# Channel attention and a top-1 mixture of experts: split weights in two places by turns, the first split two steps later, the first v loads spread over the steps of rows, one batch's first squares freed

## The chip, the cores and the metric

One Trainium2 chip, one of its cores, one program. The metric is device time in microseconds of one execution; the time of a kernel is the median of its runs. Inputs and output are float32 in the chip's memory.

## The reference

```python
def _attn_ref(q, k, v, tau):                    # B, N, C = 4, 5056, 256
    qn = q / (np.linalg.norm(q, axis=1, keepdims=True) + 1e-06)
    kn = k / (np.linalg.norm(k, axis=1, keepdims=True) + 1e-06)
    s = kn.transpose(0, 2, 1) @ qn / tau        # 256 x 256 for each batch
    a = softmax(s)                              # over the last axis
    return v @ a

def _moe_ref(x, w_gate, w_output_gate, w1, w2): # x: 20224 x 256; E = 8, F = 1024
    logits = x @ w_gate
    e_idx = np.argmax(logits, axis=1)
    probs = softmax(logits)
    gate_w = probs[np.arange(N), e_idx]
    eom = 1.0 / (1.0 + np.exp(-(x @ w_output_gate)))
    for e in range(E):
        mask = e_idx == e
        h = np.maximum(x[mask] @ w1[e], 0.0)
        out[mask] = gate_w[mask, None] * eom[mask, e, None] * (h @ w2[e])

def reference(q, k, v, tau, **moe):
    return _moe_ref(_attn_ref(q, k, v, tau).reshape(20224, 256), **moe)
```

q and k are normalised along the 5056 rows, so a batch's 256 x 256 product can be scaled after it is summed. Each of the 20224 rows then goes through the one expert of eight that its logits choose.

## The kernel before, in words

The five engines and their queues are TensorE (PE, matmuls), VectorE (DVE), ScalarE (ACT), GpSimd (POOL, which issues the indirect transfers) and SyncE (SP, which issues the direct ones). SP and POOL issue in the order of the program; a row that waits holds up all rows behind it.

**Attention.** `gram(b)` goes over one batch in 20 steps of 256 rows. A step loads its rows of q and k (L406, tile `qk`, six of them), squares them on ACT (L390), adds the squares up on DVE (L391), and multiplies on PE into `s_ps` (L429). Behind the last step the product is copied from PSUM to `s_sb` (L438), scaled and made into the softmax. `mix(b)` then goes over the rows of v: `turn` loads v (L537, half a MB each, tile `v`), PE transposes (L543) and multiplies with the softmax (L573 to L575), `st` gets the result, and `route` sends each row into the place of its expert in the buffer `xs_d`, with scatters by POOL (L651). The batches overlap: while `mix` of batch b runs, `gram` of the next one does, and some of the first v loads are issued in it.

**Experts.** The experts are ranked by their number of rows, and the sorted rows are worked off in units of 256. A unit's first product `h_part` (L996 to L998) has 48 matmuls in four steps of 12, its `hb` (ReLU on ACT, L1000, and the rest on DVE, L1001) follows for each step, and its second product `y_part` (L1020 to L1022) goes by steps as well, a unit behind; a step of the run has 12 matmuls of each kind, 24 in all. PE works in float16 with each number as a sum of two parts, high and low, hence three matmuls for one product. A unit's rows are fetched (`xg`, L918), scaled and split into `xr16` (L970, L971; one tile of tag "sq" for a pair of units, two such tiles), and transposed by transfers on SP's queue (`xt`, L975). Its result `yo` (L1026) is stored by POOL (L1033). The h products and the small product `w_ps` below use one set of four PSUM tiles.

**Weights.** Each expert's w1 and w2 are split into the two parts once. `prep` does it for ranks 1 to 7 while the run goes on: for each half (half 0 is w1, half 1 is w2) `load_raw` loads 1 MB on SP (L288) into a tile of tag "st", which the scatters must have left; `split` squares it on ACT in two pieces (L333), DVE sums (`wtot`, L338), PE multiplies by ones (`w_ps`, L339) so that each partition has the total, the scale follows, and ACT makes the high part (`whi`, L354), DVE the low part (`wlo`, L355). `keep` writes both to `wsc` in the chip's memory (L363, half a MB each, on SP). Units fetch their expert's weights from there into `wbuf` (L889, POOL). Rank 0 is split ahead of the run, in `wbuf` itself, and units 0 to 6 use it; units 7, 13, 20, 26, 33, 39 and 46 are the first that may need ranks 1 to 7.

The parts lie in one tile each, of tags "sp" and "sl" with one buffer; so a split may begin only when the `keep` before it has been written out.

**Order.** Code is written by generators that take turns, and a scheduler places each engine's instructions by simulated times. `_beside(run, (preps, rate))` advances the preps by `rate` of a step for each step of the run: SRATE for the first 20 steps, WRATE (0.45) behind them. `pause(n)` gives n turns away. `issue_after` and `behind` hold an instruction behind another one on its engine; `in_turn` holds each piece of a split behind the run's last piece on ACT, DVE and PE. `AHEADW` = 2 is how many loads of weights stand ahead of the split that is worked on.

Of the kernel before, what the change touches and what calls it, by code (L numbers as in the profile page):

```python
# [9 lines left out]
F16 = mybir.dt.float16  # L10
BF16 = mybir.dt.bfloat16
F32 = mybir.dt.float32
# [26 lines left out]
def tile_colnorm_attention_then_top1_moe(  # L39
# [87 lines left out]
    LATE = 12  # L127
    MWAIT = 12
    BRATE = 0.7
    SOON, SRATE = 20, 0.9  # L130
    WRATE = 0.45
    WAITW = 1
    RWAIT = 3
    SMALL = 9
    VAFTER = 6
    AHEADW = 2
# [152 lines left out]
        return raw  # L289

    held = []

    def prep(first, end, tag):
        todo = []
        for r in range(first, end):
            for half in range(2):
                with behind("SP"):
                    raw = load_raw(r, half, tag)
                todo.append(lambda raw=raw, half=half, r=r: in_turn(split(raw, half, r), "ACT", "DVE", "PE"))
                yield  # L300
                if len(todo) > AHEADW:
                    yield from todo.pop(0)()
        for f in todo:
            yield from f()
# [17 lines left out]
    def split(raw, half, r):  # L322

        rows = slice(r * P, (r + 1) * P)
        if r == 0:
            hi, lo = (wbuf[half][:, 0, n * HW1 : (n + 1) * HW1] for n in range(2))
        else:
            hi = big.tile([P, HW1], F16, tag="sp", name=f"whi{r}_{half}", bufs=1)
            lo = big.tile([P, HW1], F16, tag="sl", name=f"wlo{r}_{half}", bufs=1)
        ss = sm.tile([P, 2], F32, tag="wss", name="wss")  # L330
        for i in range(2):
            a = slice(i * HW1 // 2, (i + 1) * HW1 // 2)
            nc.scalar.activation(hi[:, a], raw[:, a], AF.Square, accum_out=ss[:, i : i + 1])  # L333
            yield
        yield from pause(WAITW)
        w_ps = ps_x.tile([P, 512], F32, tag="x", name="w_ps")
        tot = sm.tile([P, 1], BF16, tag="wtot", name="wtot")
        nc.vector.tensor_tensor(out=tot, in0=ss[:, 0:1], in1=ss[:, 1:2], op=ALU.add)  # L338
        nc.tensor.matmul(w_ps[:, 0:1], onesb, tot, start=True, stop=True)  # L339
        sw = sm.tile([P, 1], F32, tag="wsw", name="wsw")  # L340
        root2(w_ps[:, 0:1], KW, sw, invw[:, half, r : r + 1])

        if half == 0:
            src, dh, dl = (
                raw.rearrange("p (c m f) -> p c f m", c=CC, f=FC),
                hi.rearrange("p (c f m) -> p c f m", c=CC, f=FC),
                lo.rearrange("p (c f m) -> p c f m", c=CC, f=FC),
            )
            cuts = [(slice(None), c, slice(i, i + FC // 2)) for c in range(CC) for i in (0, FC // 2)]
        else:  # L350
            src, dh, dl = raw, hi, lo
            cuts = [(slice(None), slice(i * HW1 // 2, (i + 1) * HW1 // 2)) for i in range(2)]
        for i, a in enumerate(cuts):
            nc.scalar.activation(dh[a], src[a], AF.Copy, scale=sw)  # L354
            nc.vector.scalar_tensor_tensor(  # L355
                out=dl[a], in0=src[a], scalar=sw, in1=dh[a], op0=ALU.mult, op1=ALU.subtract
            )
            if i % 2:
                yield
        def keep():  # L360
            with behind("SP"):
                for n, part in enumerate((hi, lo)):
                    nc.sync.dma_start(wsc[half][rows, n * HW1 : (n + 1) * HW1], part)  # L363

        if r == 0:
            held.append(keep)
        else:
            keep()
        if half == 1:
            iw = invw[:, :, r : r + 1]  # L370
            nc.vector.tensor_tensor(out=iw[:, 0, :], in0=iw[:, 0, :], in1=iw[:, 1, :], op=ALU.mult)
            prepped.append(r)
# [5 lines left out]
    def gram(b):  # L378
# [14 lines left out]
        for st in range(nstep):  # L393
            t0 = TS * st
            last = st == nstep - 1
            qk = ld.tile([P, 2, TS, C], F32, tag="qk", name=f"qk{b}_{st}", bufs=QKB)
            for i, src in enumerate((q, k)):
                main = src[b, :MAIN].rearrange("(p t) c -> p t c", p=P)
                nt = TS - 1 if last else TS
                if last and REM < P:  # L400
                    nc.vector.memset(qk[REM:, i, TS - 1, :], 0.0)
                if b == 0 and st == 0:
                    for t in range(nt):
                        (nc.sync, nc.scalar)[i].dma_start(qk[:, i, t, :], main[:, t, :])
                    continue
                load = nc.sync.dma_start(qk[:, i, :nt, :], main[:, t0 : t0 + nt, :])  # L406
                if b == 1 and st == VAFTER:
                    mile["rows"] = load
                if last:
                    nc.sync.dma_start(qk[:REM, i, TS - 1, :], src[b, MAIN:])  # L410
            for t0 in range(0, TS, 2):
                qp = qk[:, :, t0 : t0 + 2, :]
                if not last:
                    with ExitStack() as held_back:
                        if st < 2 and "copy" in mile:
                            held_back.enter_context(tc.issue_after(mile["copy"].ins))
                        squares(st, t0, qp)
                if b in WHOLE:
                    terms = [(qp, qp)]
                else:  # L420
                    hi = wk.tile([P, 2, 2, C], F32R, tag="qkh", name=f"qkh{b}_{st}_{t0}")
                    nc.scalar.copy(hi, qp)
                    lo = wk.tile([P, 2, 2, C], F32R, tag="qkl", name=f"qkl{b}_{st}_{t0}")
                    nc.vector.tensor_tensor(out=lo, in0=qp, in1=hi.bitcast(F32), op=ALU.subtract)
                    terms = [(hi, hi), (hi, lo), (lo, hi)]
                for t in range(2):
                    for c in range(CC):
                        for n, (kt, qt) in enumerate(terms):
                            nc.tensor.matmul(  # L429
                                s_ps[:, c, :], kt[:, 1, t, c * P : (c + 1) * P], qt[:, 0, t, :],  # L430
                                start=st == 0 and t0 == 0 and t == 0 and c == 0 and n == 0,
                                stop=last and t0 == TS - 2 and t == 1 and n == len(terms) - 1,
                                skip_group_check=True,
                            )
                yield
# [90 lines left out]
    def turn(b, j):  # L526
# [3 lines left out]
        if i % 2 == 0:  # L530
# [2 lines left out]
            vt = ld.tile([P, 4, C], F32, tag="v", name=f"v{b}_{g}_{i}", bufs=VB)  # L533
            with ExitStack() as held_back:
                if b == 0 and g < 2:
                    held_back.enter_context(tc.issue_after(mile["rows"].ins))
                main(SP=nc.sync.dma_start(vt[:np_], vg[:, 2 * i : 2 * i + 4, :]))  # L537
            sts["v"] = vt
        vp = sts["v"][:, 2 * (i % 2) : 2 * (i % 2) + 2, :]
# [618 lines left out]
```

## Time and profile before

| | us |
|---|---|
| median of three runs | 1213.61 (1211.7 to 1219.58) |
| the profiled execution | 1205.79 |
| its span | 1204.0 |
| PE busy | 1172.7 (97%) |
| DVE busy | 710.7 (59%) |
| ACT busy | 625.5 (52%) |
| POOL busy | 565.5 (47%) |

The granted clock of TensorE was 0.995 over the span. The profiled execution is 7.8 us under the median of the runs. Attention and routing take about the first 366 us, with the run of the experts beginning beside its end; the rest is the run. In rows of the profile, L12 is line 12 of the kernel; a wait is put down to the semaphore that came last; numbers of tiles are left out of names, so `raw` is any of the weights' loads, and `whi` any of the high parts.

### The profile page before, as it was taken

To read this page: it belongs to the slowest core of one execution; us is meant where nothing else is said; L and a number is where in the kernel's file an instruction comes from. 1 tells how busy PE (TensorE), PEld (TensorE's weight loads), DVE (VectorE), ACT (ScalarE), POOL (GpSimd) and SP (SyncE) were. 2 spreads that over 40 slices of the span, in tenths; PEclk is the share of its full clock that TensorE was granted. 3 is DMA by queue.
4 is the path that set the end of the run, shared out by engine and by line. 5 is a ranking of instruction groups with operands and counts; after the bars stand their busy time and mean duration, and the time that the engine had idled before them with its cause. 6 is when DMAs were issued, how large, how long until landed. Compare 5 with 4: busy or idle time off the path is not lost.

```text
span 1204.0 us, 27760 instructions
## 1 busy us (share of the span) xinstructions
PE 1172.7 (97%) x10412; PEld 1061.5 (88%) x10412; DVE 710.7 (59%) x2123; ACT 625.5 (52%) x1233; POOL 565.5 (47%) x561
## 2 busy tenths in 40 slices
PE   8999999999898899999999999999999999999998
PEld 7899899999787788888888888888889999999997
DVE  6676757758895655465565656544445555555551
ACT  5576757657746555465555555433333344344442
POOL 0004574767575235544444554445555544444443
PEclk9999999999999899999999999999999999999999
DMA  8986787847689855665655545733335433337843
GB/s 301 326 294 226 254 273 252 301 153 266 191 256 295 211 151 151 147 147 151 139 147 150 139 126 158 195 77 77 77 69 170 116 73 80 77 78 205 183 115 131
DMA packets 174882, 208.54 MB, mean 173 GB/s; under 512 B 120936, under 2 KB 124526, under 8 KB 169752
## 3 DMA queue, kind: packets, MB, share of 16 engines
q1 hardware_dynamic: 130312, 126.58, 37.3%
q0 software_dynamic: 43312, 79.73, 22.9%
q8 instruction: 84, 1.38, 0.5%
q14 instruction: 54, 0.44, 0.1%
q10 hardware_dynamic: 1120, 0.42, 0.1%
HBM read 275.55 MB, written 61.41 MB: 280 GB/s over the span
## 4 chain that ended last, share of the span: by engine, by line
PE 64%; issue 16%; DMA 8%; POOL 7%; ACT 3%; DVE 1%; POOLq 0%; SPq 0%; ACTq 0%; DVEq 0%
PE s_ps L429 8%; PE h_ps L996 8%; PE h_ps L998 8%; PE h_ps L997 8%; PE y_ps L1020 8%; PE y_ps L1022 8%; PE y_ps L1021 8%; POOL out_dram L1033 4%; DMA qk<-in_k_dram 2%; PE x_ps L573 2%; PE x_ps L575 2%; PE x_ps L574 2%; PE vt_ps L543 2%; POOL wbuf L889 2%; DMA xs_d<-st,r_si 2%
## 5 line engine op out<-in xcount | busy, mean ns | idle before, releaser
L1001 DVE SCALAR_TENSOR_TENSOR hb<-h_ps,hb 128x512 f16<-128x512 f32 (+1 forms) x360 | 227.8, 636 | 330.3 <-ACT hb L1000 329.9
L1000 ACT ACTIVATE hb<-h_ps 128x512 f16<-128x512 f32 (+1 forms) x360 | 196.9, 551 | 341.3 <-PE h_ps L998 340.9
L996 PE MATMUL h_ps<-xt,wbuf 128*128 128x256 f16 (+1 forms) x1440 | 367.9, 263 | 3.7 <-ACT st L576 2.0
L998 PE MATMUL h_ps<-xt,wbuf 128*128 128x256 f16 (+1 forms) x1440 | 368.0, 263 | 0.0
L997 PE MATMUL h_ps<-xt,wbuf 128*128 128x256 f16 (+1 forms) x1440 | 367.8, 263 | 0.0
L1020 PE MATMUL y_ps<-wbuf,hb 128*128 128x256 f16 x1296 | 353.4, 273 | 1.1 <-DMA wbuf<-wsc,wi 1.1
L1021 PE MATMUL y_ps<-wbuf,hb 128*128 128x256 f16 x1296 | 353.4, 273 | 0.0
L1022 PE MATMUL y_ps<-wbuf,hb 128*128 128x256 f16 x1296 | 353.2, 273 | 0.0
L889 POOL DMA_INDIRECT wbuf<-wsc,wi x166 | 168.9, 1018 | 221.0 <-PE h_ps L998 163.1
L651 POOL DMA_INDIRECT xs_d<-st,r_si x160 | 173.0, 1081 | 180.5 <-ACT st L576 106.1
L1033 POOL DMA_INDIRECT out_dram<-yo,b_id x162 | 166.7, 1029 | 69.0 <-issue 41.2
L996 PEld LDWEIGHTS <-wbuf 128*128 128x128 f16 x1440 | 141.4, 98 | 18.8 <-DMA wbuf<-wsc,wi 2.6
L997 PEld LDWEIGHTS <-wbuf 128*128 128x128 f16 x1440 | 141.4, 98 | 14.7 <-issue 0.4
L429 PE MATMUL s_ps<-qk 128*128 128x256 f32 x640 | 148.1, 384 | 5.9 <-DMA qk<-in_q_dram 3.9
L998 PEld LDWEIGHTS <-wbuf 128*128 128x128 f16 x1440 | 141.4, 98 | 14.1
L1021 PEld LDWEIGHTS <-hb 128*128 128x128 f16 x1296 | 126.7, 98 | 15.3 <-issue 1.2
L1022 PEld LDWEIGHTS <-hb 128*128 128x128 f16 x1296 | 126.7, 98 | 14.9 <-DVE hb L1001 0.2
L1020 PEld LDWEIGHTS <-hb 128*128 128x128 f16 x1296 | 126.7, 98 | 14.2 <-ACT hb L1000 0.3
L429 PEld LDWEIGHTS s_ps<-qk 128*128 128x128 f32 x640 | 119.6, 192 | 21.4 <-DMA qk<-in_k_dram 3.9
L905 POOL DMA_INDIRECT xg<-xs_d,gi x49 | 50.8, 1036 | 155.2 <-DVE xr L971 145.8
L391 DVE TENSOR_TENSOR acc<-acc,sq 128x1024 f32<-128x1024 f32 x76 | 92.9, 1223 | 36.9 <-ACT sq L390 29.8
L390 ACT ACTIVATE sq<-qk 128x1024 f32<-128x1024 f32 x76 | 80.1, 1061 | 44.7 <-DMA qk<-in_k_dram 39.1
(195 smaller groups left out, 1488.4 us busy)
## 6 DMA issues: line engine op xcount, KB each, us to landing
qk<-in_q_dram SPq DMA_DIRECT2D x75, 256.0 KB
qk<-in_k_dram SPq DMA_DIRECT2D x75, 256.0 KB
v<-in_v_dram SPq DMA_DIRECT2D x32, 512.0 KB
raw<-in_moe_w_dram SPq DMA_DIRECT2D x16, 1024.0 KB
xg<-xs_d SPq DMA_DIRECT2D x30, 272.0 KB
wsc<-whi SPq DMA_DIRECT2D x14, 512.0 KB
wsc<-wlo SPq DMA_DIRECT2D x14, 512.0 KB
v<-in_v_dram SPq DMA_DIRECT2D x8, 480.0 KB
```

The source lines that it names most:

```text
L429: nc.tensor.matmul(s_ps[:, c, :], kt[:, 1, t, c * P : (c + 1) * P], qt[:, 0, t, :], start=st == 0 and t0 == 0 and t == 0 and c == 0 and n ...
L651: ins = nc.gpsimd.indirect_dma_start(out=xs_d[:, :], out_offset=bass.IndirectOffsetOnAxis(ap=si[:np_, t : t + 1], axis=0), in_=st[:np_, t, ...
L889: nc.gpsimd.indirect_dma_start(out=wbuf[half][:, at_of(u), :], out_offset=None, in_=wsc[half][:end, :], in_offset=bass.IndirectOffsetOnAxi ...
L996: nc.tensor.matmul(hp, w1s[:, 0, c, fs], xh, start=fi == 0 and c == 0, stop=False, **KWM)
L997: nc.tensor.matmul(hp, w1s[:, 0, c, fs], xl, start=False, stop=False, **KWM)
L998: main(PE=nc.tensor.matmul(hp, w1s[:, 1, c, fs], xh, start=False, stop=fin, **KWM))
L1000: main(ACT=nc.scalar.activation(hh, h_ps[:, :, :w], AF.Relu))
L1001: ins = nc.vector.scalar_tensor_tensor(out=hb[:, 1, 2 * fp : 2 * fp + 2, :w], in0=h_ps[:, :, :w], scalar=0.0, in1=hh, op0=ALU.max, op1=ALU ...
L1020: nc.tensor.matmul(y_ps[:, t, :], hb[:, 0, f, tsl], w2s[:, 0, f, :], start=st, stop=False, **KWM)
L1021: nc.tensor.matmul(y_ps[:, t, :], hb[:, 0, f, tsl], w2s[:, 1, f, :], start=False, stop=False, **KWM)
L1022: main(PE=nc.tensor.matmul(y_ps[:, t, :], hb[:, 1, f, tsl], w2s[:, 0, f, :], start=False, stop=fin, **KWM))
L1033: ins = nc.gpsimd.indirect_dma_start(out=out[:, :], out_offset=bass.IndirectOffsetOnAxis(ap=un["id"][:, t : t + 1], axis=0), in_=un["yo"][ ...
```

## The change

Five edits. (1) The preps advance by one step for each step of the run rather than by 0.9, in the first 20 steps. (2) Rank 1's two splits are each given two turns later (PWAIT), behind the loads. (3) The parts of half 0 keep one place of tags "sp" and "sl", and the parts of half 1 get another: `whi2` takes one of the two "sq" tiles and `wlo2` the tile "acc" of the attention's squares. Both places are allocated once and held until rank 7, so that `xr16` has one "sq" tile left in that time. (4) The first four v loads of batch 0 follow the rows of steps 6, 8, 10 and 12 of batch 1 rather than all those of step 6. (5) From batch 1 on, the squares of steps 0 and 1 no longer wait for the copy `s_sb` of the batch before, while those of steps 2 and 3 now do.

```diff
-    SOON, SRATE = 20, 0.9
+    SOON, SRATE = 20, 1.0
...
+    PWAIT = 2
...
+    parts_of = {}
...
                 if len(todo) > AHEADW:
+                    if r == first + 1:
+                        yield from pause(PWAIT)
                     yield from todo.pop(0)()
...
         else:
-            hi = big.tile([P, HW1], F16, tag="sp", name=f"whi{r}_{half}", bufs=1)
-            lo = big.tile([P, HW1], F16, tag="sl", name=f"wlo{r}_{half}", bufs=1)
+            if half not in parts_of:
+                if half == 0:
+                    parts_of[half] = [
+                        big.tile([P, HW1], F16, tag=tag, name=name, bufs=1) for tag, name in (("sp", "whi"), ("sl", "wlo"))
+                    ]
+                else:
+                    parts_of[half] = [
+                        pool.tile([P, 2, 2, C], F32, tag=tag, name=name, bufs=n)
+                        .bitcast(F16)
+                        .rearrange("p i t c -> p (i t c)")
+                        for pool, tag, name, n in ((wk, "sq", "whi2", 2), (one, "acc", "wlo2", 1))
+                    ]
+            hi, lo = parts_of[half]
...
-                if b == 1 and st == VAFTER:
-                    mile["rows"] = load
+                if b == 1:
+                    mile[st] = load
...
-                        if st < 2 and "copy" in mile:
+                        if 2 <= st < 4 and "copy" in mile:
                             held_back.enter_context(tc.issue_after(mile["copy"].ins))
                         squares(st, t0, qp)
...
                 if b == 0 and g < 2:
-                    held_back.enter_context(tc.issue_after(mile["rows"].ins))
+                    held_back.enter_context(tc.issue_after(mile[VAFTER + 2 * (2 * g + i // 2)].ins))
```

Lines behind the first edit move: L288, L333, L339, L354, L363, L406, L537, L970, L975, L1000 and L1026 of before are L289, L348, L354, L369, L378, L421, L552, L985, L990, L1015 and L1041 after.

What stands on SP's queue at the seam of batches 0 and 1, before. `qk_7` is the tile of batch 1's step 7, `v_0_2` the v load of batch 0's group 0, from its row block 2 on:

```order
L406 DMA qk_7_485<-in_q_dram 128x512
L406 DMA qk_7_485<-in_k_dram 128x512
L537 DMA v_0_0_557<-in_v_dram 128x1024
L537 DMA v_0_2_577<-in_v_dram 128x1024
L406 DMA qk_8_502<-in_q_dram 128x512
L406 DMA qk_8_502<-in_k_dram 128x512
L537 DMA v_1_0_650<-in_v_dram 128x1024
L537 DMA v_1_2_755<-in_v_dram 128x1024
L406 DMA qk_9_512<-in_q_dram 128x512
L406 DMA qk_9_512<-in_k_dram 128x512
```

After, at the same place:

```order
L552 DMA v_0_0_557<-in_v_dram 128x1024
L421 DMA qk_7_485<-in_q_dram 128x512
L421 DMA qk_7_485<-in_k_dram 128x512
L421 DMA qk_8_502<-in_q_dram 128x512
L421 DMA qk_8_502<-in_k_dram 128x512
L552 DMA v_0_2_577<-in_v_dram 128x1024
L421 DMA qk_9_512<-in_q_dram 128x512
L421 DMA qk_9_512<-in_k_dram 128x512
L421 DMA qk_10_522<-in_q_dram 128x512
L421 DMA qk_10_522<-in_k_dram 128x512
L552 DMA v_1_0_650<-in_v_dram 128x1024
```

The v loads now stand two steps of rows apart; the fourth follows `qk_12`. `qk_8` has one of them ahead of it rather than two, `qk_9` two rather than four, and `qk_7` one rather than none.

SP's queue where rank 1's weights are loaded, before. `raw_0` is w1 and `raw_1` w2; the transposes are those of units 4 and 5, and TENSOR_LOAD and ISA read the expert's number:

```order
L918 DMA xg<-xs_d 128x544
L975 DMA_TRANSPOSE xt<-xr_5070 128x4x128 x2
L284 TENSOR_LOAD ri
L288 ISA
L288 DMA raw_0_5078<-in_moe_w_dram 128x2048
L284 TENSOR_LOAD ri
L288 ISA
L288 DMA raw_1_5110<-in_moe_w_dram 128x2048
L975 DMA_TRANSPOSE xt<-xr_5070 128x4x128 x2
```

After:

```order
L933 DMA xg<-xs_d 128x544
L285 TENSOR_LOAD ri
L289 ISA
L289 DMA raw_0_5030<-in_moe_w_dram 128x2048
L990 DMA_TRANSPOSE xt<-xr_5075 128x4x128 x2
L285 TENSOR_LOAD ri
L289 ISA
L289 DMA raw_1_5083<-in_moe_w_dram 128x2048
L990 DMA_TRANSPOSE xt<-xr_5075 128x4x128 x2
```

The load of w1 went ahead of unit 4's transposes; w2's stays between those of units 4 and 5. Further on, the writes of w2's parts (`wsc` from `whi2` and `wlo2`) moved as well: before they stood behind the load of rank 3's w1 and ahead of unit 8's transposes, after they stand behind those and ahead of that load.

ACT at the splits of rank 1's w2 (`raw_1`) and rank 2's w1 (the second `raw_0`), before:

```order
L1000 ACTIVATE hb<-h_ps 128x512
L333 ACTIVATE whi_1_5458,wss<-raw_1_5110 128x1024 x2
L1026 ACTIVATE yo<-y_ps,b_gs 128x256 x2
L354 ACTIVATE whi_1_5458<-raw_1_5110,wsw 128x1024 x2
L1000 ACTIVATE hb<-h_ps 128x512 x4
L1026 ACTIVATE yo<-y_ps,b_gs 128x256 x2
L970 ACTIVATE xr_5732<-xg,b_sx 128x256 x2
L1000 ACTIVATE hb<-h_ps 128x512 x2
L333 ACTIVATE whi_0_5740,wss<-raw_0_5145 128x1024 x2
L1000 ACTIVATE hb<-h_ps 128x512
```

After:

```order
L348 ACTIVATE whi_5565,wss<-raw_1_5083 128x1024
L985 ACTIVATE xr_5382<-xg,b_sx 128x256 x2
L1015 ACTIVATE hb<-h_ps 128x512
L1041 ACTIVATE yo<-y_ps,b_gs 128x256 x2
L1015 ACTIVATE hb<-h_ps 128x512
L369 ACTIVATE whi_5565<-raw_1_5083,wsw 128x1024 x2
L1015 ACTIVATE hb<-h_ps 128x512 x2
L348 ACTIVATE whi,wss<-raw_0_5115 128x1024
L1015 ACTIVATE hb<-h_ps 128x512
L348 ACTIVATE whi,wss<-raw_0_5115 128x1024
```

The squares of rank 2's w1 stand behind `hb` 23 and 24 of the run rather than 26, and write `whi`, the place of rank 1's w1, rather than that of the split just ahead of them. On PE, `w_ps` of rank 1's w1 has 156 matmuls of `h_ps` and 143 of `y_ps` ahead of it (before 144 and 144), that of its w2 252 and 226 (240 and 226), that of rank 2's w1 348 and 322 (324 and 300), and the last one 1920 and 1894 (1896 and 1872). The first split's squares stand on ACT behind the 12th `hb` in both.

## The prediction

> **What bounds the kernel now.** I read the page's first two parts, then the waits of TensorE (PE), then windows around each wait, then the chain that ended last.
>
> ```profile
> PE 1172.7 (97%) x10412; PEld 1061.5 (88%) x10412; DVE 710.7 (59%) x2123; ACT 625.5 (52%) x1233; POOL 565.5 (47%) x561
> PEclk9999999999999899999999999999999999999999
> ```
>
> PE is busy for 1172.7 of 1204.0 us. The change takes away no matmul, so all that it can win is the 31 us in which PE stands still, and whatever PE loses to a lower clock: the granted clock has one slice with an 8, the fourteenth of 30.1 us each, 391 to 421 us. PE's largest waits, over the whole span (total, times, longest):
>
> ```profile
> PE w_ps L339 <- DVE wtot L338: 9.1, 4, 4.8
> PE s_ps L429 <- DMA qk<-in_q_dram: 3.9, 1, 3.9
> PE s_ps L429 <- DMA qk<-in_k_dram: 2.0, 2, 1.5
> PE h_ps L996 <- DMA wbuf<-wsc,wi: 1.6, 1, 1.6
> ```
>
> The 3.9 us is the first load of the kernel, which stays. The 9.1 us is nearly all in two stalls at the matmul of a weight's sum of squares; the 2.0 us is at the seam of batches 0 and 1. In time (start, duration, and in brackets the idle time before it):
>
> ```profile
> 366.14 0.18 PE L339 MATMUL w_ps<-wtot,onesb 128*128 128x1 bf16 x1 [4.82 <-DVE wtot L338]
> 408.70 0.18 PE L339 MATMUL w_ps<-wtot,onesb 128*128 128x1 bf16 x1 [3.97 <-DVE wtot L338]
> 55.83 1.96 PE L429 MATMUL s_ps<-qk 128*128 128x256 f32 x8 [0.46 <-DMA qk<-in_k_dram]
> 59.77 8.87 PE L429 MATMUL s_ps<-qk 128*128 128x256 f32 x40 [1.54 <-DMA qk<-in_k_dram]
> ```
>
> DVE's sum `wtot` is only the last link. ACT shows what came late:
>
> ```profile
> 363.70 1.06 ACT L333 ACTIVATE whi<-raw 128x1024 f16<-128x1024 f32 x1 [6.75 <-DMA raw<-in_moe_w_dram]
> 383.98 1.06 ACT L333 ACTIVATE whi<-raw 128x1024 f16<-128x1024 f32 x1 [0.91 <-DMA wsc<-whi]
> 405.18 1.06 ACT L333 ACTIVATE whi<-raw 128x1024 f16<-128x1024 f32 x1 [6.37 <-DMA wsc<-whi]
> ```
>
> The first stall waits for the load of rank 1's w1. The second (the first split of rank 2) waits until the one place for the parts, `whi`, has been written out to `wsc`. From the square to the stalled matmul is 366.14 − 363.70 = 2.44 us both times, within 1.1 us.
>
> **What the stalls cost.** Windows of 10 us; PE's busy time is followed by its matmuls in brackets, and after POOL comes the granted clock.
>
> ```profile
> 350.00:360.00 10.00, 10.00 (x94) 8.95 (x93) 9.20 (x46) 2.99 (x7) 7.87 (x8) 1.00 1.03 308
> 360.00:370.00 10.00, 5.18 (x34) 3.71 (x32) 2.49 (x6) 6.11 (x10) 7.85 (x8) 0.83 1.11 304
> 400.00:410.00 10.00, 6.03 (x52) 4.93 (x50) 2.90 (x15) 4.40 (x10) 1.75 (x2) 0.86 0.95 288
> 410.00:420.00 10.00, 10.00 (x75) 8.22 (x74) 7.69 (x16) 6.51 (x9) 2.42 (x3) 0.80 0.76 165
> 367.00:368.00 1.00, 1.00 (x7) 0.69 (x5) 0.00 (x0) 1.00 (x2) 0.97 (x1) 0.50 1.23 149
> 55.00:60.00 5.00, 3.00 (x13) 2.08 (x12) 1.22 (x1) 1.32 (x2) 0.00 (x0) 1.00 1.04 395
> ```
>
> An undisturbed window has 94 matmuls in 10 us, 0.106 us each. Around the first stall there are 34: 60 missing, 60 × 0.106 = **6.4 us**, of which 4.82 are idle and the rest is half clock (0.50 at 367 us). Around the second, 42 + 19 = 61 are missing: **6.5 us**, 3.97 of them idle. The seam's idle 0.46 + 1.54 = **2.0 us** left the clock at 1.00. So a long stall costs more than its idle time, a short one not.
>
> The Trainium skill, "TensorE: Matmul & The Clock Gate", Part 1, says that the array falls to half clock after an idle window of about 3.4 us and returns to full after a busy one. The rows agree at 4.82, 3.97 and 1.54 us; by it a stall cut below a window also gives its slow stretch back, as in the sum here.
>
> **The change, part by part.**
>
> *Rank 1's first load (the first stall).* In the order after, SP issues rank 1's w1 right behind the two gathers `xg` and ahead of unit 4's pair of transposes.
>
> ```profile
> 349.25 1.79 SPq L918 DMA_DIRECT2D xg<-xs_d  x2
> 351.15 3.66 SPq L975 DMA_TRANSPOSE xt<-xr  x2
> 355.85 3.44 SPq L288 DMA_DIRECT2D raw<-in_moe_w_dram  x2
> 355.85 7.83 DMA raw<-in_moe_w_dram
> ```
>
> The last row is from the chain: 7.83 us from issue to landing. Before, the issue follows the transposes' end (351.15 + 3.66 = 354.81) by 1.04 us. The same gap behind the gathers gives 351.04 + 1.04 = 352.1, landing at 359.9 and the matmul ready at 359.9 + 2.44 = 362.3. PE now comes to it 11 matmuls later (156 h and 143 y matmuls ahead of it, before 144 and 144): 366.14 − 4.82 + 11 × 0.106 = 362.5. So there is no wait, by a hair. Bounds: all 6.4 us won; or the load lands no earlier than 363.7, and PE waits 366.1 − 362.5 = 3.6 us, so 2.8 are won or less. I take 6.0, as a small rest costs no clock. PWAIT itself moves nothing on ACT here: the squares still stand behind the 12th `hb`. The displaced transposes then land at about 363.7 at the latest, where the load landed. Unit 4 needs them four steps after the 12th `hb`; a step is the distance of the first two of these rows, 2.62 us, and the third is the 12th:
>
> ```profile
> 349.57 0.60 ACT L1000 ACTIVATE hb<-h_ps 128x512 f16<-128x512 f32 x1 [2.02 <-PE h_ps L998]
> 352.19 0.60 ACT L1000 ACTIVATE hb<-h_ps 128x512 f16<-128x512 f32 x1 [2.02 <-PE h_ps L998]
> 355.33 0.57 ACT L1000 ACTIVATE hb<-h_ps 128x512 f16<-128x512 f32 x1
> ```
>
> So they are needed at 355.3 + 4 × 2.62 = 365.8: cover of 2 us.
>
> *Two places (the second stall).* Rank 2's first split takes the place of rank 1's w1, not of w2.
>
> ```profile
> 380.94 0.57 SPq L363 DMA_DIRECT2D wsc<-whi  x1
> 394.07 0.65 SPq L363 DMA_DIRECT2D wsc<-whi  x1
> 393.63 0.34 SPq L288 DMA_DIRECT2D raw<-in_moe_w_dram  x1
> 394.07 11.04 DMA wsc<-whi
> ```
>
> Those are the two writes before: w1's was through by 383.98 (3.0 us), w2's took 11.04, behind the 1 MB load issued at 393.63. After, the squares of that split stand behind `hb` 23 and 24, at 355.3 + 11 × 2.62 = 384 and later, and the place is free at 384 even if the write goes no earlier than before. The matmul stands behind 348 h matmuls, 29 steps, at 355.3 + 17 × 2.62 = 400. So PE does not wait: **6.5 us**. The bad end is w2's 11.04 for this write: 381 + 11 + 2.4 = 394, still ahead of 400, so both ends give 6.5, and this term is the safest.
>
> *What the second place costs.* It is one of the two "sq" tiles, which `xr16` used by turns. Now a pair of units may write its rows only when the pair before has been transposed. The first place where it counts is units 8 and 9: ACT wrote `xr` there at 395.48; unit 7's transposes were issued from 386.61 to 391.27 and land 2.3 us later (from the chain), at 393.6: about 2 us of cover. If it fails, ACT stands, and the `hb` behind it; with four tiles of h in PSUM, PE follows about a step and a half later. I put it at 0 (bound: 2 us here, and the rival below for all pairs).
>
> ```profile
> 395.48 0.91 ACT L970 ACTIVATE xr<-xg,b_sx 128x256 f16<-128x256 f32 x2 [0.35 <-DVE b_sx L254]
> 386.61 4.66 SPq L975 DMA_TRANSPOSE xt<-xr  x2
> 440.77 2.31 DMA xt<-xr
> SPq L975 <- DVE xr L971: 528.9, 82, 14.7
> ```
>
> The last row is SP's wait over the whole kernel: transposes wait for rows, 82 times, not rows for transposes, which speaks for the 0.
>
> *SRATE.* Splits go at one step each rather than 0.9; the last split's matmul stands 24 matmuls later, 2 steps or 5 us, at step 160 of the run (unit 40), and rank 7 is first needed at unit 46. Nothing.
>
> *v loads and squares at the seam.* Half a MB, a v load, is 1.3 us at the 395 GB/s of 55 to 60 us.
>
> ```profile
> 45.90 0.90 SPq L537 DMA_DIRECT2D v<-in_v_dram  x2
> 48.10 2.32 SPq L537 DMA_DIRECT2D v<-in_v_dram  x2
> 51.14 8.49 DMA qk<-in_k_dram
> ```
>
> qk_8, late by 0.46, has one v load less ahead of it; qk_9, late by 1.54, has two less, 2.6 us. Both stalls go: 2.0 us. qk_7 has one v more ahead, 1.3 us; PE did not wait for it, but its margin is not shown, so 0 to 1.3 come back. Freed squares only fill ACT's wait. I take 1.5.
>
> **The sum.** 6.0 + 6.5 + 1.5 = 14.0. For new small waits anywhere in an order that moved I take nothing in the middle, and ±4 at the ends (two waits of the kind of the `wbuf` row above, and as much that may go). The profiled execution took 1205.8 us (span 1204.0 and 1.8 around it), so about 1192 under the profiler. The three runs shown have their median 7.8 higher; I subtract from that: 1213.6 − 14.0 = 1199.6, **1200 us**. About one per cent is what a measurement of this kernel can tell from no change (the runs shown lie 0.65% apart), so 1200 is a change just beyond that.
>
> **The rivals.**
>
> *The first stall stays.* The load is issued earlier but lands as late, because rank 0's weights, four writes of half a MB, and the gathers are ahead of it:
>
> ```profile
> 344.53 3.58 SPq L363 DMA_DIRECT2D wsc<-wbuf  x4
> ```
>
> The Trainium skill, "DMA: Bandwidth & Descriptors", Queues, rings and completion order, says that an engine works off a queue's descriptors in their order; by it the load passes the transposes but not the writes.
>
> The DMA share of 1.03 at 350 to 360 us speaks for this rival; against it, that the transposes it passes are the last thing issued ahead of it. Then PE waits 3.6 us again, long enough for some of the slow clock, and of the 6.0 some 1 is won: 1199.6 + 5 gives **1205**.
>
> *w2 of unit 7 comes late.* Its write now stands behind unit 8's transposes, which need `xr` written behind `hb` 25, at 355.3 + 13 × 2.62 = 389.4; 0.9 for the rows and 4.66 as above give an issue at about 395, and 3 to 11 us to land. The fetch took up to 8.8 us:
>
> ```profile
> 741.07 8.78 DMA wbuf<-wsc,wi
> ```
>
> 395 + 3 + 1 + 8.8 = 408, or 416 with the 11. PE wants it 403 h matmuls into the run, at 355.3 + 21.6 × 2.62 = 411.9. The write now stands ahead of the next 1 MB load rather than behind it, which speaks for 3. If not, PE stands 4 us and the clock falls: 4 to 6.5 back, **1205**.
>
> *Slower: the single tile for `xr16`.* If transposes land more than a unit's four steps (10.5 us) after their rows are written, ACT, and with it every `hb`, waits at each pair of units until the last split:
>
> ```profile
> L354 ACT ACTIVATE whi<-raw,wsw x42: 1132/1209/1242, 366.8 to 759.7; 128x512 f16<-128x512 f32 x28, 128x1024 f16<-128x1024 f32 x14
> ```
>
> That is (760 − 367) / 21 = 19 pairs. SP's queue carries the writes of parts as well, and one such row delays a pair by 3 to 11 us; the step and a half of cover is 4. Of the 0 to 7 us beyond it I take 1.5 a pair, 28 in all: 1199.6 + 28 = **1228**. The point from which it decides: ACT's rows L985 wait for `xt<-xr` more than 4 us each. Against it: the 2.31 us from issue to landing.
>
> The Trainium skill, "Trainium Kernel Development and Optimization", Best Practices, recommends double buffers to overlap transfers with work, which this edit gives up for `xr16`; the 528.9 us of SP waiting for rows say that the second one was hardly used.
>
> *Nothing to see.* New waits of the same kind as the ones removed: DVE is at 9.20 of 10 at 350 to 360 us, and a split moved into a busy stretch may delay `hb`. Then 1208 to 1217, **1212**.
>
> **How the numbers follow.** Forecast 0.56 (its own range 1195 to 1204), first stall stays 0.14, w2 late 0.11, slower by `xr16` 0.08, nothing to see 0.11. The likeliest gives 1200. 1193 is the forecast with 4 more won and the median's own spread; 1210 takes in the two rivals at 1205 and half of the last. Faster by over 1% means below 1201.5: some three quarters of the forecast and a little of the rivals, 0.45; slower by over 1%, above 1225.7: most of the `xr16` case, 0.07; the rest, 0.48, within.
>
> **What will show it.** PE's row `w_ps <- wtot` falls from 9.1 below 1.5 us, no slice of the clock is below 9 but for the first, and 360 to 370 and 400 to 420 us have over 90 matmuls in 10 us. Of `s_ps <- qk` only the 3.9 us at the start stay. Wrong would be: `w_ps` still waiting 3 us at 362 (first rival), `y_ps <- wbuf` near 412 (second), or ACT's L985 behind `xt<-xr` (third).

## The result and the profile after

The changed kernel takes 1203.14 us (median of 16 runs), the one before 1213.76 (16 runs); the ratio is 0.9928, 95% interval 0.9901 to 0.9956: 8.7 us won, 5.3 to 12.0. That is 5 us short of the 14 in the sum, which lies outside the interval. The median is inside the forecast's own range, 1195 to 1204, by 0.9 us; 8.7 off the 1213.6 from which the prediction subtracts gives 1204.9, just above it. So the hit is in part luck. Ratios and intervals, here and below, leave out the runs more than 1.5% above the fastest of the same kernel; on the chip where the kernel before takes 1295.6 us these are 6 of the changed kernel's 12 and 13 of the 35 before, so that its ratios are less sure. The profiled execution took 1198.0 us (span 1196.3), 7.7 less than that of before; it is the fastest of the 16.

PE's waits after (total, times, longest), to be read against the same list of before:

```profile
PE s_ps L444 <- DMA qk<-in_q_dram: 3.9, 1, 3.9
PE y_ps L1035 <- DMA wbuf<-wsc,wi: 3.1, 2, 1.7
PE h_ps L1011 <- ACT st L591: 2.9, 1, 2.9
PE w_ps L354 <- DVE wtot L353: 2.5, 3, 2.1
PE vt_ps L558 <- DVE vl L564: 1.8, 3, 1.1
PE s_ps L444 <- DMA qk<-in_k_dram: 0.9, 2, 0.6
```

The wait at `w_ps` fell from 9.1 to 2.5, but not below 1.5. PE's waits for `wbuf` (weights fetched for a unit) sum to 3.1 rather than 2.7 us, and those for `vl` (the low part of v) to 1.8 rather than 0.7. Before, beside the 1.6 us of `h_ps`, these two rows stood:

```profile
PE y_ps L1020 <- DMA wbuf<-wsc,wi: 1.1, 1, 1.1
PE vt_ps L543 <- DVE vl L549: 0.7, 2, 0.5
```

The windows of the two stalls, after:

```profile
350.00:360.00 10.00, 10.00 (x94) 8.97 (x92) 9.98 (x46) 3.42 (x7) 7.80 (x7) 1.00 0.99 330
360.00:370.00 10.00, 7.86 (x58) 6.17 (x56) 3.82 (x9) 6.32 (x9) 7.64 (x8) 0.83 1.15 280
400.00:410.00 10.00, 10.00 (x95) 8.96 (x93) 4.83 (x20) 4.22 (x8) 2.23 (x3) 1.00 1.03 273
410.00:420.00 10.00, 8.64 (x80) 7.60 (x79) 9.20 (x20) 7.34 (x12) 7.11 (x6) 1.00 0.74 207
```

The first stall still lacks 36 of 94 matmuls (60 before) and has the clock at 0.83 as before: 24 × 0.106 = 2.5 us won. Of the second, 61 missing became 14, and those have another cause: 5.0 us won. Together 7.5, nearly all of the difference of the spans. What stood there, first a row of PE (start, duration, idle time before it):

```profile
365.69 0.18 PE L354 MATMUL w_ps<-wtot,onesb 128*128 128x1 bf16 x1 [2.14 <-DVE wtot L353]
PE y_ps L1035 <- DMA wbuf<-wsc,wi: 1.4, 1, 1.4
```

The second row is PE's wait for unit 7's w2, from its waits at 380 to 420 us.

This is the account of one good execution. A second profile of the changed kernel ("changed, again" below, 1204.96 us, span 1203.2) has 4.46 us at the first stall and 2.2 at unit 7. From 350 to 430 us, in the same windows of 10 us, PE has 633 matmuls there, 704 in the first profile, and 632 in the kernel before, whose profiled execution is itself 7.8 us under its median. What the change wins is therefore told by the ratios; the profiles show which waits came and went.

### The profile page after: what moved, and what is told of

It reads as the page before. It is cut to its first block, busy times and chain, and to the rows that moved or that the text cites. A ratio compares the mean times of both kernels' runs of the same rounds, so it can differ in the third digit from the quotient of the medians.

```text
span 1196.3 us, 27750 instructions
## 1 busy us (share of the span) xinstructions
PE 1170.8 (98%) x10412; PEld 1060.2 (89%) x10412; DVE 711.5 (59%) x2123; ACT 623.4 (52%) x1233; POOL 572.7 (48%) x561
## 4 chain that ended last, share of the span: by engine, by line
PE 67%; issue 14%; POOL 8%; DMA 6%; ACT 2%; DVE 2%; SPq 1%; POOLq 0%; ACTq 0%; DVEq 0%
PE s_ps L444 9%; PE h_ps L1011 8%; PE h_ps L1013 8%; PE h_ps L1012 8%; PE y_ps L1037 8%; PE y_ps L1035 8%; PE y_ps L1036 8%; POOL out_dram L1048 4%; POOL wbuf L904 3%; PE x_ps L588 3%; PE x_ps L590 3%; PE x_ps L589 3%; PE vt_ps L558 2%; DMA qk<-in_k_dram 2%; DMA xt<-xr 1%
## 5 line engine op out<-in xcount | busy, mean ns | idle before, releaser
L1015 ACT ACTIVATE hb<-h_ps 128x512 f16<-128x512 f32 (+1 forms) x360 | 197.2, 552 | 343.1 <-PE h_ps L1013 342.6
L904 POOL DMA_INDIRECT wbuf<-wsc,wi x166 | 171.3, 1032 | 220.2 <-PE h_ps L1013 166.4
L1048 POOL DMA_INDIRECT out_dram<-yo,b_id x162 | 169.9, 1049 | 64.4 <-issue 42.1
L406 DVE TENSOR_TENSOR acc<-acc,sq 128x1024 f32<-128x1024 f32 x76 | 93.1, 1225 | 45.8 <-ACT sq L405 39.9
```

Source lines behind the costliest of these rows:

```text
L904: nc.gpsimd.indirect_dma_start(out=wbuf[half][:, at_of(u), :], out_offset=None, in_=wsc[half][:end, :], in_offset=bass.IndirectOffsetOnAxi ...
L1015: main(ACT=nc.scalar.activation(hh, h_ps[:, :, :w], AF.Relu))
L1048: ins = nc.gpsimd.indirect_dma_start(out=out[:, :], out_offset=bass.IndirectOffsetOnAxis(ap=un["id"][:, t : t + 1], axis=0), in_=un["yo"][ ...
```

## The experiments

The experiments ran on three chips. On two of them every kernel, that of before included, takes 70 to 82 us more. A good part of that is lost between 100 and 400 us: PE is busy 258.2 of these 300 us in the profile of the two places alone, 287.6 in that of the kernel before. What causes it was not settled. So each kernel is compared with the kernel before on its own chip; the last column tells the chips apart.

| | ratio to before | 95% interval | before, us |
|---|---|---|---|
| two places alone | 0.9949 | 0.9915 to 0.9984 | 1282.9 |
| SRATE and PWAIT alone | 0.9992 | 0.9954 to 1.0030 | 1282.9 |
| seam alone | 1.0005 | 0.9965 to 1.0045 | 1282.9 |
| changed, early load | 0.9877 | 0.9816 to 0.9938 | 1282.9 |
| changed, again | 0.9950 | 0.9919 to 0.9981 | 1213.3 |
| changed, w2's part in v | 0.9878 | 0.9838 to 0.9918 | 1213.3 |
| changed, early load, again | 0.9894 | 0.9864 to 0.9925 | 1213.3 |
| changed, both | 0.9905 | 0.9874 to 0.9936 | 1213.3 |
| changed, a third time | 0.9964 | 0.9916 to 1.0012 | 1295.6 |
| changed, PWAIT 3 | 0.9967 | 0.9938 to 0.9996 | 1295.6 |
| two places, early load | 0.9888 | 0.9849 to 0.9926 | 1295.6 |
| changed, w2's part in v, again | 1.0007 | 0.9974 to 1.0040 | 1295.6 |

**The edits one by one.** The kernel before with `parts_of` alone:

```diff
-            hi = big.tile([P, HW1], F16, tag="sp", name=f"whi{r}_{half}", bufs=1)
-            lo = big.tile([P, HW1], F16, tag="sl", name=f"wlo{r}_{half}", bufs=1)
...
+            hi, lo = parts_of[half]
```

> The kernel before with the third edit alone: the parts of w1 and of w2 have a place each, and nothing else changes. Theory (the gain is the two stalls at w_ps, each with its own edit): the second stall goes (61 missing matmuls, 6.5 us, less 1.5 if w2 of unit 7 comes late as it did after), the first stays as before (4.8 us idle, 34 matmuls in 360 to 370 us), so -5 to -6.5 us. Rival (the places are not what matters; the later splits move both stalls away): the second stall stays near 4 us and the time within 1 us of before.

The ratio is 0.9949, 6.5 us (2.1 to 10.9). ACT never waits for `wsc<-whi` here. With one place it does, in the kernel before (first row) and in the run of the seam's edits alone, on the same chip as this one (second row). PE's waits at `w_ps` with two places are short (third row):

```profile
ACT whi L333 <- DMA wsc<-whi: 23.3, 11, 6.4
ACT whi L333 <- DMA wsc<-whi: 20.0, 9, 5.0
PE w_ps L351 <- DVE wtot L350: 3.2, 5, 1.0
```

The first stall is not to be seen on this chip (ACT waits 1.6 us for the load), so the rows say nothing of the first term. At rank 2's first split PE waits for nothing, where the seam's edits alone leave it 2.60 us. The place alone gives about as much as the whole change; 2.60 us is less than half of the 6.5, and no row was found for the rest.

The first two edits alone:

```diff
-    SOON, SRATE = 20, 0.9
+    SOON, SRATE = 20, 1.0
...
+    PWAIT = 2
...
+                    if r == first + 1:
+                        yield from pause(PWAIT)
```

> The kernel before with the first two edits alone: SRATE 1.0 and the two turns of PWAIT, one place for the parts, the seam as before. Theory: the first stall falls from 4.8 to about 2 us as after (2 to 3 us won with the clock); at the second split the place is still taken by w2's parts, but their write is issued earlier (ahead of the next load of 1 MB rather than behind it), the squares stand behind hb 28 instead of 26 and the matmul 24 matmuls later, so that stall shrinks to 0 to 3 us instead of 4: -4 to -7 us in all. Rival (only a second place removes it): the second stall stays near 4 us, -2.5 us in all.

Nothing that can be told from none: −1.0 us, −5.9 to +3.9. The single place is still felt by ACT at the splits, and PE has a wait for weights:

```profile
ACT whi L337 <- DMA wsc<-whi: 8.6, 5, 3.1
PE h_ps L1000 <- DMA wbuf<-wsc,wi: 4.4, 1, 4.4
```

The waits at `w_ps` shrank (2.3 us in 5 places, none at rank 2's first split), as the theory said and the rival did not. The 4 to 7 us that were to come of it are not seen, though the interval reaches 5.9. The 4.4 us at `wbuf` stand at 1003.7 us, long behind the splits of rank 1, and no run ties them to these edits. So on this chip the second stall could go without a gain that shows, and what a second place wins beyond that stall stays open.

The last two edits alone:

```diff
-                if b == 1 and st == VAFTER:
-                    mile["rows"] = load
+                if b == 1:
+                    mile[st] = load
...
-                        if st < 2 and "copy" in mile:
+                        if 2 <= st < 4 and "copy" in mile:
...
-                    held_back.enter_context(tc.issue_after(mile["rows"].ins))
+                    held_back.enter_context(tc.issue_after(mile[VAFTER + 2 * (2 * g + i // 2)].ins))
```

> The kernel before with the last two edits alone: v loads at steps 6, 8, 10 and 12, squares of steps 0 and 1 freed and those of 2 and 3 held. Theory (the seam gives back what it wins): PE's waits for qk between 50 and 70 us fall from 2.0 to about 0.9 us, and a wait of about 1 us for vl takes their place as after: within 1 us of before. Rival (the forecast's term): -1.5 to -2 us in the profile's first 100 us. In the time neither can be told from none; the profile's waits up to 110 us decide.

The ratio is 1.0005. PE's waits from 50 to 110 us, of this kernel:

```profile
PE vt_ps L543 <- DVE vl L549: 1.1, 1, 1.1
PE s_ps L429 <- DMA qk<-in_k_dram: 0.3, 1, 0.3
```

So 1.7 of the 2.0 us at qk go (the two places alone, with the old order on the same chip, have 2.0 as well), and 1.1 come back at `vl`. The chain of the changed kernel (start, duration) shows why `vl` is late: a load of k that landed at 65.7, the squares that wait for it and those behind them, and three of DVE's additions ahead of `vl`.

```profile
59.10 6.62 DMA qk<-in_k_dram
65.82 1.06 ACT sq L405
...
72.97 1.22 DVE acc L406
74.28 1.23 DVE acc L406
76.03 1.22 DVE acc L406
77.24 0.61 DVE vl L564
77.90 0.66 PE vt_ps L558 x4
```

**The first stall.** One line in the changed kernel takes one step of the preps ahead of the four writes of rank 0's parts. It issues rank 1's first load there, and it puts the loads and splits behind it a step earlier as well:

```diff
+    next(preps)
     for keep in held:
         keep()
```

> The changed kernel with the first load of rank 1's w1 issued ahead of the four writes of rank 0's parts instead of behind them (one step of the preps taken before those writes). Theory (the first stall is left because the load lands late, and DVE's sum behind an hb adds 1.1 us): the load lands near 354, the squares stand behind hb 9 and 10, the matmul waits for nothing, the clock stays at 1.00 in 360 to 370 us with 94 matmuls instead of 58: 3.8 us less than the changed kernel, about -12 us against before. Rival (the load's place in the queue does not matter, since the tile that it needs comes free late, or the work that it passes is late instead): the same time as the changed kernel, with a new wait of PE for xt or wbuf of some 2 to 4 us.

> The changed kernel with the first load of rank 1's w1 ahead of the writes of rank 0's parts, once more beside the changed kernel itself. Theory (the first stall's rest is the load and DVE's order): 3.8 us less than the changed kernel, no wait at the first w_ps, clock 1.00 there. Rival (a chip on which all engines often stand hid it in the run before, and the gain of 1.2% there is not the load): the same as the changed kernel within 1 us.

The ratios are 0.9877 and 0.9894. The second stands beside the changed kernel on one chip (0.9950, intervals that overlap by a hair):

> The changed kernel itself, so that the next three stand beside it on one chip. Expected as before: 0.5 to 1% faster than the kernel before, w_ps waits about 2 us at the first split with the clock at half behind it, y_ps waits about 1.4 us for wbuf at unit 7.

SP, ACT and PE of the changed kernel there, then of that with the early load:

```profile
354.21 0.33 SPq L289 DMA_DIRECT2D raw<-in_moe_w_dram  x1
364.37 1.06 ACT L348 ACTIVATE whi<-raw 128x1024 f16<-128x1024 f32 x1 [6.51 <-DMA raw<-in_moe_w_dram]
367.89 0.19 PE L354 MATMUL w_ps<-wtot,onesb 128*128 128x1 bf16 x1 [4.46 <-DVE wtot L353]
```

```profile
346.16 0.36 SPq L289 DMA_DIRECT2D raw<-in_moe_w_dram  x1
353.72 1.06 ACT L348 ACTIVATE whi<-raw 128x1024 f16<-128x1024 f32 x1 [5.50 <-DMA raw<-in_moe_w_dram]
373.04 0.27 PE L1011 MATMUL h_ps<-xt,wbuf 128*128 128x256 f16 x1 [2.93 <-DVE b_ix L258]
```

In the changed kernel the load took 7.95 us in one execution and 10.2 in another, and the stall was 2.14 and 4.46, before 4.82: it was never removed. With the load issued eight us earlier it is gone. The load itself took 7.56 us there, ahead of the writes, little less than the 7.95 behind them, so beside the first profile it was the earlier issue that told.

The line moves more than the load. The squares stand behind the 9th and 10th `hb` rather than the 12th, and the matmul has 144 and 129 matmuls ahead of it rather than 156 and 143. The write of w2's parts stands ahead of unit 8's transposes again, and is issued at 390.78 rather than at 405.04:

```profile
390.78 0.41 SPq L378 DMA_DIRECT2D wsc<-whi  x1
```

In place of the stall PE waits 2.93 us at the first product of a unit (put down to DVE's `b_ix`; in the run with both edits a wait of 1.7 us at that place is put down to the transposes `xt<-xr`), and 2.5 for `hb`. From 350 to 390 us this profile lacks 72 of 376 matmuls, the changed kernel's first profile 35 and its second 80. From 390 to 430, where unit 7's wait was, it lacks 1, the other two 13 and 39. So beside the second profile the gain lies at unit 7 more than at the first stall.

Against the changed kernel the ratio differs by 0.0056 of 1213, about 7 us, between none and 14 by the two intervals. The theory's 3.8 us agree with that; its 94 matmuls and full clock at 360 to 370 us came only in part (79 matmuls, clock 1.00, and a window at half clock from 373.5 us). Which part of the line pays was not separated.

> The changed kernel with PWAIT 3 instead of 2: PE has 168 h and 148 y matmuls ahead of the first w_ps (156 and 143 before), so it comes there 17 matmuls or 1.8 us later. Theory (the first stall is the load's landing, 8 to 10 us after its issue, and every step that the matmul is put off takes off 2 us of it): the wait at the first w_ps falls from 2 to 4.5 us to 0 to 2.5 us; but the write of w1's parts now stands behind the load of rank 2's w2 and that of w2's parts behind the load of rank 3's w1, so that unit 7's fetches land 4 to 8 us later and PE waits for wbuf at unit 7 by 3 to 8 us: slower than the changed kernel by 0 to 6 us. Rival (the more room the better): 2 to 4 us faster than the changed kernel.

This was the other way to meet the stall: 0.9967, the same as the changed kernel beside it (0.9964). The medians of all the runs are 1288.0 and 1296.9, so whether it is a little faster is open; slower, as the theory had it, it is not. It has long waits at `wbuf`:

```profile
PE h_ps L1011 <- DMA wbuf<-wsc,wi: 4.9, 1, 4.9
PE y_ps L1035 <- DMA wbuf<-wsc,wi: 2.8, 1, 2.8
```

But they stand at 1014 and 841 us and not at unit 7, where the theory had them, and the changed kernel on this chip has one of 3.0 us at 827 us too.

> The changed kernel itself, beside the next three. Expected 0.4 to 0.8% faster than the kernel before, with 2 to 4.5 us of waiting at the first w_ps, as in its two runs so far.

On this chip the stall at the first `w_ps` was 0.7 us, so neither the 2 to 4.5 us nor what PWAIT 3 takes from them could be seen there. What the early load wins on such a chip (below) is then hardly the first stall.

**The second place and `xr16`.** In the changed kernel ACT waits for the single "sq" tile three times; this is the first:

```profile
397.91 0.91 ACT L985 ACTIVATE xr<-xg,b_sx 128x256 f16<-128x256 f32 x2 [3.37 <-DMA xt<-xr]
399.00 2.52 SPq L990 DMA_TRANSPOSE xt<-xr  x2
401.57 0.57 SPq L378 DMA_DIRECT2D wsc<-whi  x1
408.50 1.01 POOL L904 DMA_INDIRECT wbuf<-wsc,wi  x1 [5.43 <-DVE wsw L269]
```

Rows, transposes, the write of w2's parts and unit 7's fetch stand in a row behind it, and PE waits 1.4 us for the fetch (the idle time before it is put down to `wsw`; in the second profile that of the same fetch is put down to the write, `wsc<-wlo`). With w2's high part in a tile of v:

```diff
-                        for pool, tag, name, n in ((wk, "sq", "whi2", 2), (one, "acc", "wlo2", 1))
+                        for pool, tag, name, n in ((ld, "v", "whi2", VB), (one, "acc", "wlo2", 1))
```

> The changed kernel with w2's high part in one of the four tiles of v (free by then) instead of in an 'sq' tile, so that xr16 has its two tiles again; the order of PE, ACT and SP around the splits is the same. Theory (the single tile holds up unit 8's rows by 3.4 us, with them its transposes, the write of w2's parts behind them and the fetch for unit 7): ACT's xr no longer waits for xt<-xr (13.8 us in three places before), the write of w2's parts goes about 3 us earlier, and PE's 1.4 us at y_ps of unit 7 is gone: 1 to 2 us less than the changed kernel. Rival (the tile does not matter, the write is late for its place in the queue): the waits of xr go, but y_ps still waits 1 us or more, same time.

```profile
396.32 0.92 ACT L985 ACTIVATE xr<-xg,b_sx 128x256 f16<-128x256 f32 x2
400.24 0.57 SPq L378 DMA_DIRECT2D wsc<-whi  x1
PE y_ps L1035 <- DMA wbuf<-wsc,wi: 1.3, 1, 1.3
```

ACT's wait is gone, the write goes 1.3 us earlier, and PE's wait stays, as the rival had it. The rival's reason is not shown, though: unit 7's fetch is issued 2.9 us earlier and then takes longer. In the changed kernel, then here (start, duration):

```profile
408.50 8.46 DMA wbuf<-wsc,wi
405.56 13.21 DMA wbuf<-wsc,wi
```

Why it took longer is open. The ratio was 0.9878 all the same, with a profiled execution slower than the changed kernel's on this chip (span 1205.8 against 1203.2; a wait for `wbuf` at 760 us is 6.5 us there). So it was run again:

> The changed kernel with w2's high part in a tile of v, once more. Its first run was 0.7% faster than the changed kernel beside it, but its profile shows the same stall at the first w_ps (4.0 us) and the same wait at unit 7 (1.3 us). Theory (the tile moves only waits of ACT that PE does not feel, so the 0.7% was the scatter of executions): within 0.4% of the changed kernel. Rival (xr16's second tile does pay over the nineteen pairs of units): 0.5% or more faster than the changed kernel again.

1.0007, beside 0.9964 of the changed kernel: on this other chip the gain did not come again. The 1.2%, from six runs, was most likely the scatter of executions, which its interval did not cover; that the chip matters is not excluded.

> Both: the first load ahead of rank 0's writes, and w2's high part in a tile of v. If the two act apart, the sum of both: 5 to 6 us less than the changed kernel. If they share a cause (both only move the write of w2's parts forward), no more than the larger of the two.

0.9905, no more than the early load alone (0.9894) on the same chip, so the tile adds nothing there either.

**A shorter version.** The two places and the early load on the kernel before, without the other three edits:

> The kernel before with two edits: the two places, and the first load of rank 1's w1 ahead of the writes of rank 0's parts; no PWAIT, SRATE 0.9, the seam as before. Theory (two places take away the second stall, the early load the first, and the rest of the change gives nothing): both w_ps waits are gone, 1.0 to 1.3% faster than the kernel before, the same as or better than the changed kernel with the early load (0.9 to 1.2%). Rival (the later splits are needed too): a wait at w_ps or xt of 3 us or more near the first split, and 0.5% or less.

0.9888 (0.9849 to 0.9926), beside 0.9964 (0.9916 to 1.0012) of the changed kernel on the same chip; the medians of all the runs are 1278.8 and 1296.9. PE's waits at `w_ps` there sum to 1.5 us:

```profile
PE w_ps L351 <- DVE wtot L350: 1.5, 3, 0.8
```

With two edits it beats the kernel before clearly, and by these figures the changed kernel too, though the intervals overlap by a hair. Whether it beats the changed kernel with the early load is open (they never ran on one chip).

## Why the prediction was right, and where not

The sign and the place were right, and the median lies in the range. Of the three terms, one held. Of the four signs that were to show the forecast, one came in full in the first profile: no slice of the clock is below 9. `w_ps` kept 2.5 us, 360 to 370 us has 58 matmuls and 410 to 420 us 80, and 0.9 us stays at qk.

*Rank 1's first load, 6.0 us.* It gave 2.5 in the first profile, so its own rival ("The first stall stays") took more than half; in the second it gave nothing that can be seen (220 matmuls from 350 to 380 us, 222 before). The rival's reason, a load that lands as late behind the four writes, is not in the first profile: from issue to squares the load took about what it took before. In the second, with 10.2 us, it may be. In the first profile the step had four numbers, and three were short. PE came to the matmul at 363.55; the start of the run was 1.0 us later than before, which moves both sides. The gathers came 0.4 us later still, and the load was issued 1.8 us behind them instead of 1.04, at 354.2 instead of 353.1: 1.1. Issue to the squares took 7.95 instead of 7.83: 0.1. The square to the matmul took 365.69 − 362.14 = 3.55 instead of 2.44:

ACT's row and DVE's rows there:

```profile
364.23 0.57 ACT L1015 ACTIVATE hb<-h_ps 128x512 f16<-128x512 f32 x1
364.84 0.69 DVE L1016 SCALAR_TENSOR_TENSOR hb<-h_ps,hb 128x512 f16<-128x512 f32 x1 [4.56 <-ACT hb L1015]
365.44 0.19 DVE L353 TENSOR_TENSOR wtot<-wss 128x1 bf16<-128x1 f32 x1
```

The matmul moved behind the 13th step on PE, and `wtot` moved behind that step's `hb` on DVE, which waits for ACT's `hb`, which stands behind the squares: 1.1 us. That is the piece that the sum had left out: I moved the matmul by 11 matmuls on PE and its input by nothing. The prediction's own rows had warned of it. Its "2.44 us both times, within 1.1 us" was 2.44 at the first stall and 408.70 − 405.18 = 3.52 at the second, where an `hb` stood behind the squares already, and it took the smaller. 1.1 + 0.1 + 1.1 less the margin of 0.2 is the wait of 2.1.

*Two places, 6.5 us.* Held: no wait at rank 2's matmul, in either profile of the changed kernel or in that of the place alone. That the place alone won just 6.5 us is in part chance: its interval is 2.1 to 10.9, and on that chip the stall with one place was 2.60 us. Of the parts that ran alone it is the only one with an effect that can be told from none.

*w2 of unit 7.* The rival came, at 1.4 us rather than 4 to 6.5; in the second profile it was 2.2, with a window at half clock behind it. The write was issued at 401.57 rather than at about 395, and the fetch at 408.50 rather than 399; the fetch's 8.46 us were as estimated (8.8). A part of that is the "sq" tile. I had unit 7's transposes landing 2.3 us behind their issue, at 393.6; by ACT's wait for them they landed at 397.9, 8.5 us behind the end of their issue. Two writes, 1 MB of load and three gathers were issued just ahead of them, which is the likely reason; the DMA share at 380 to 390 us is 0.98. The 2.31 us was a row from a quiet stretch of the queue (share 0.33 at 440 to 450 us, before). But the tile alone does not explain PE's wait, which stayed at 1.3 us without it. The slower rival, 1.5 us for each of 19 pairs of units, did not come: ACT waits three times (13.8 us in all), and from 420 to 1190 us PE is idle no longer than before (2.9 us against 3.3).

*The seam, 1.5 us.* Nothing: qk's wait fell from 2.0 to 0.9, and 1.1 came at `vl`. The loads were put in another order, their number stayed: a later step pays, through the squares and DVE rather than through PE's own wait, and I had followed the loads only as far as PE.

*The clock.* That "a long stall costs more than its idle time, a short one not" fell, below: the 2.14 us that were left cost clock.

## What to carry to other kernels

Here a stall went away when the transfer that ends it was issued eight us earlier, and not when its consumer was moved by 11 matmuls: look at what the issue of the load stands behind in its queue, and how far it can be moved past that. When an instruction is moved on one engine, follow its inputs through the order of the other engines too, since they move behind other work as well. A transfer's latency is read from a row with as much ahead of it in the queue as it will have, not from the chain's shortest row. And a sum of windows from one profile is checked against a second profile of the same kernel before a gain is put down to a wait: here 7.5 us in one was nothing in the other.

## What the runs showed of the hardware

An idle time of 2.14 us was enough for half clock. Three windows of 3.41 us of the changed kernel (behind the window's length PE's busy time, third from the end the granted clock), then two of its second run:

```profile
362.98:366.39 3.41, 1.27 (x14) 0.89 (x12) 1.17 (x5) 1.87 (x6) 2.80 (x3) 1.00 1.03 328
366.39:369.80 3.41, 3.41 (x19) 2.43 (x17) 2.20 (x3) 3.41 (x4) 2.54 (x3) 0.50 1.07 264
369.80:373.21 3.41, 3.41 (x33) 3.06 (x32) 3.41 (x8) 3.41 (x7) 2.81 (x2) 1.00 1.07 399
```

```profile
420.41:423.82 3.41, 1.20 (x12) 0.94 (x10) 3.34 (x10) 1.56 (x4) 2.93 (x2) 1.00 0.86 313
423.82:427.23 3.41, 3.41 (x18) 2.37 (x17) 0.87 (x3) 0.60 (x1) 0.00 (x0) 0.50 0.81 136
```

The clock changes on a grid of 3.41 us that runs on by itself: in the second run half clock begins at 324.8, 365.8 and 423.8 us, 12 and 17 windows apart. A window with 1.27 or 1.20 us busy is followed by one at half clock, and a full one brings the clock back. One that still holds 0.85 us of idle time does not: with w2's part in v, the first stall of 3.95 us was followed by 6.8 us at half clock. A longer idle time that the grid cuts in two costs nothing: 2.94 us at 324 us in the changed kernel left 2.00 and 1.89 us busy in its two windows, at full clock.

```profile
322.02:325.43 3.41, 2.00 (x16) 1.81 (x16) 1.90 (x8) 0.00 (x0) 2.50 (x4) 1.00 1.07 276
325.43:328.85 3.42, 1.89 (x17) 1.82 (x18) 0.78 (x5) 1.93 (x8) 2.68 (x3) 1.00 0.46 174
```

The Trainium skill, "TensorE: Matmul & The Clock Gate", Part 1, has the free-running window and half clock after an idle one. The window agrees; that it must be idle as a whole does not, and here the measurement decides. So a stall of 2 to 3 us costs 1.7 us more (half of one window) or nothing, by where the grid falls. That may be part of the scatter from run to run; how much was not measured.
